# Rewriting a fused attention and expert-routing kernel: batched routing, plain loads, interleaved head pairs, independent scatters

## The chip, the cores and the metric

The kernel runs on one core of one Trainium2 chip. The metric is the device time of one execution in microseconds (us). PE is the matmul engine, PEld its weight loads, ACT the scalar engine, DVE the vector engine, Pool (POOL) the general-purpose engine, SP the engine that only issues DMAs. "Clock" is the share of full speed that was granted to PE, by the clock records of the trace; the time before the first record is counted as 1.00.

## The reference, cut to what matters

Eight batches, eight heads, 576 tokens, head size 64. Each head adds two attentions: a coarse one over means of four tokens, repeated four times, and a local one in which a token sees the seven tokens around it. The result has 4608 rows of 512. Then each row goes through the two-layer network of its domain (one of eight experts).

```python
q_d = q.reshape(B, H, Sd, factor, D).mean(axis=3)           # k_d, v_d alike; factor = 4
out_up = np.repeat(sm_attn(q_d, k_d, v_d), factor, axis=2)
mask = np.abs(pos[:, None] - pos[None, :]) < factor
out_local = softmax(np.where(mask, scale * q @ k.T, -1e9)) @ v
x = (out_up + out_local) as rows of tokens                   # 4608 x 512
for e in range(E):                                           # 8 experts
    m = domain_id == e
    out[m] = np.maximum(x[m] @ w1[e], 0.0) @ w2[e]           # 512 -> 1024 -> 512
```

## The kernel before

Attention works on pairs of heads. It loads q, k and v with converting DMAs from Pool (256 bytes of fp32 become 128 bytes of fp16), loads v once more in overlapping windows, and writes local rows and coarse rows to DRAM. After every second batch a pass reads both back, adds them, and writes the sum.

```python
for src, dst, dstl in ((q, qn, qnl), (k, kn, knl), (v, vq, vql)):
    nc.gpsimd.dma_start(dst[:], src[b, hA:hA+2, 0:512, :].rearrange("h (p r) d -> p r h d", r=4))
    ...
# _od_add_pass, 36 times in all, DMAs issued from ACT
nc.scalar.dma_start(xt[:], xdr[base:base+P, :])
nc.scalar.dma_start(ot[:], odb[srow:srow+32, :].unsqueeze(1).broadcast_to([32, 4, DM]))
nc.vector.tensor_add(xt[:], xt[:], ot[:])
nc.scalar.dma_start(xdr[base:base+P, :], xt[:])
```

Routing computes the place of each token in its expert's list in 36 serial steps on DVE and PE, and 36 indirect DMAs write the list to DRAM. The expert stage has room for 6 x 128 tokens per expert; each block of 128 output rows is scattered to its tokens.

```python
for j in range(CAPJ):                                     # CAPJ = 6
    for fc in range(NFC):
        nc.tensor.matmul(o_ps[:], ht[:, fc, bass.ts(j, P)], w2e[:, fc, :], ...)
    o_sb = msb.tile([P, DM], FP32, name="o_sb", tag="o_sb")       # three buffers
    nc.scalar.copy(out=o_sb[:], in_=o_ps[:])
    nc.gpsimd.indirect_dma_start(out=out[:], out_offset=..idxt[:, j:j+1].., in_=o_sb[:], ...)
```

The softmax here doesn't subtract the row's maximum and nothing guards it: scores larger than these inputs give would overflow.

## Time and profile before

The time before was 688.0 us (median of 4 runs). The stages, read from the timeline of the profiled execution (691.2 us):

| stage | from, to | us |
|---|---|---|
| start, to the first score matmul | 0 to 72.8 | 72.8 |
| attention, to the last local product | to 379.0 | 306.2 |
| hand-over, to the first hidden matmul | to 414.4 | 35.4 |
| experts, to the last output matmul | to 681.2 | 266.8 |
| tail | to 691.2 | 10.0 |

Page of the kernel before, its 40 slices of time: busy tenths of PE, its clock, the mean busy share of the 16 DMA engines, and what they moved.

```profile
PE   1778989876987478866897019793939394867983
PEclk9999999999999999999999999996969788797998
DMA  9990769999999989999313597456565536363411
GB/s 119 180 82 1 56 91 95 158 142 135 118 140 138 157 116 88 119 193 185 41 30 106 134 212 165 102 85 139 97 137 98 122 82 98 110 113 119 92 60 54
```

The same by windows of time. Columns: window, its length, busy time of PE, PEld, DVE, ACT and POOL with instruction counts, clock, DMA share, GB/s.

```profile
68.00:395.00 327.00, 251.01 (x2046) 157.05 (x2045) 204.68 (x866) 161.10 (x378) 186.35 (x248) 1.00 0.91 118
410.00:691.00 281.00, 198.11 (x1087) 103.63 (x1084) 0.00 (x0) 101.77 (x144) 99.05 (x103) 0.87 0.50 106
```

In attention no engine is saturated, but the DMA engines look nearly so. The clock of 1.00 there is not a measurement: the first clock record of this trace lies at 418.5 us. The spacing of matmuls says what the clock was. Two groups of 128-column transposes, in attention and in the experts, and a 512- and a 256-column matmul before and after that record (start us, duration us, engine, line, operation, tile, shapes, count; a wait stands in brackets):

```profile
217.09 0.61 PE L272 MATMUL pdt_ps<-id16a,qn 128*128 128x128 f16 x4
416.91 0.63 PE L445 MATMUL h_ps<-xt,w1e 128*128 128x512 f16 x1
417.34 0.42 PE L449 MATMUL h_ps<-xt,w1e 128*128 128x256 f16 x1
420.04 0.38 PE L445 MATMUL h_ps<-xt,w1e 128*128 128x512 f16 x1
420.25 0.27 PE L449 MATMUL h_ps<-xt,w1e 128*128 128x256 f16 x1
459.42 0.78 PE L433 MATMUL xt_ps<-id,xg 128*128 128x128 f16 x11
```

From one start to the next, 512 columns take 0.43 us at 416.9 and 0.21 us at 420.0. Transposes come every (0.61 - 0.31) / 3 = 100 ns in attention and every (0.78 - 0.22) / 10 = 56 ns in the experts (0.31 and 0.22 us are the durations of a single one). So PE ran at about half clock through all of attention before, and its 251 us of busy time are at half clock. Mean clocks of whole executions and of windows leave this early time out.

In the experts everything has slack, and PE's row goes up and down with its clock. The list of waits of the kernel before says why. Columns: who waited, for whom, total us, times, longest.

```profile
ACT o_sb L463 <- DMA out_dram<-o_sb,idxt: 69.2, 11, 12.7
PE o_ps L458 <- ACT o_sb L463: 69.0, 21, 12.6
POOL xg L416 <- DMA idxt<-hx_idx: 44.0, 5, 9.5
```

The first two lines are one chain: PE waits for the copy of the output block, and the copy waits for a buffer that an earlier scatter still holds. The third is Pool's own wait, for the index loads of the gathers.

### The profile page before, as it was taken

Reading aid. Unit: us, or ns where it says so; the run is one execution under the profiler, and the core shown is the slowest. Engines: PE = TensorE matmul, PEld = TensorE weight load, DVE = VectorE, ACT = ScalarE, POOL = GpSimd, SP = SyncE. Lnnn points to the kernel's source line nnn. Section 1 sums busy time; section 2 is a strip of 40 time slices with the busy share of each in tenths; the row PEclk is TensorE's granted clock in tenths of the full one; section 3 lists DMA queues with packets and bytes.
Section 4 is the critical chain, followed back from the end, with each engine's and each line's share of the span. In section 5 each row is a group of like instructions: output and inputs, shape, how many; then the busy total and the mean of one; then the engine's idle time right before and its main releaser. Section 6 shows DMA issues by size and latency. Waiting matters only on the chain. (4 is left out here: it accounts for less than half of the span.)

```text
span 691.2 us, 10101 instructions
## 1 busy us (share of the span) xinstructions
PE 493.7 (71%) x3352; PEld 300.3 (43%) x3352; DVE 237.3 (34%) x1118; ACT 267.8 (39%) x528; POOL 334.2 (48%) x408
## 2 busy tenths in 40 slices
PE   1778989876987478866897019793939394867983
PEld 1777656543654245534554015441515152433441
DVE  1664455775666656667567100000000000000000
ACT  0100766425763255623764005441424152434441
POOL 9930667775975659954200155124252434243222
PEclk9999999999999999999999999996969788797998
DMA  9990769999999989999313597456565536363411
GB/s 119 180 82 1 56 91 95 158 142 135 118 140 138 157 116 88 119 193 185 41 30 106 134 212 165 102 85 139 97 137 98 122 82 98 110 113 119 92 60 54
DMA packets 226905, 77.93 MB, mean 113 GB/s; under 512 B 196609, under 2 KB 218898, under 8 KB 226836
## 3 DMA queue, kind: packets, MB, share of 16 engines
q0 software_dynamic: 133504, 46.71, 55.4%
q1 hardware_dynamic: 72100, 15.23, 12.8%
q10 hardware_dynamic: 21248, 15.35, 7.8%
q8 instruction: 26, 0.43, 0.3%
q14 instruction: 27, 0.22, 0.2%
HBM read 88.09 MB, written 23.37 MB: 161 GB/s over the span
## 5 line engine op out<-in xcount | busy, mean ns | idle before, releaser
L458 PE MATMUL o_ps<-w2e,ht 128*128 128x512 f16 x384 | 100.1, 407 | 70.3 <-ACT o_sb L463 69.0
L464 POOL DMA_INDIRECT out_dram<-o_sb,idxt x48 | 47.3, 986 | 120.4 <-ACT o_sb L463 40.8
L458 PEld LDWEIGHTS <-ht 128*128 128x128 f16 x384 | 39.5, 103 | 119.5 <-issue 87.4
L445 PE MATMUL h_ps<-xt,w1e 128*128 128x512 f16 x256 | 88.8, 394 | 1.9 <-ACT xt L438 1.0
L463 ACT COPY o_sb<-o_ps 128x512 f32<-128x512 f32 x48 | 28.1, 585 | 137.7 <-DMA out_dram<-o_sb,idxt 69.2
L416 POOL DMA_INDIRECT xg<-hx_bridge,idxt x48 | 46.3, 964 | 60.7 <-DMA idxt<-hx_idx 44.0
L449 PE MATMUL h_ps<-xt,w1e 128*128 128x256 f16 x256 | 72.0, 281 | 0.0
L230 POOL DMA_DIRECT2D qn<-in_q_dram x32 | 48.4, 1512 | 36.5 <-PE pdtl_ps L274 23.7
L230 POOL DMA_DIRECT2D vq<-in_v_dram x32 | 58.5, 1840 | 13.4 <-DVE pos_s L125 8.6
L453 ACT ACTIVATE ht<-h_ps 128x768 f16<-128x768 f32 x64 | 51.7, 811 | 28.8 <-PE h_ps L449 28.7
L149 POOL DMA_INDIRECT hx_idx<-tok_s,pos_s x36 | 37.6, 1044 | 50.1 <-DMA hx_idx<-tok_s,pos_s 45.3
L330 ACT ACTIVATE el<-sc_ps 128x640 f16<-128x640 f32 x64 | 44.7, 703 | 23.4 <-PE sc_ps L313 12.0
L230 POOL DMA_DIRECT2D kn<-in_k_dram x32 | 50.2, 1569 | 3.7 <-PE pdtl_ps L274 3.2
L313 PE MATMUL sc_ps<-qt,kt 64*128 64x128 f16 x320 | 45.4, 303 | 9.2 <-POOL kt L268 4.6
L262 ACT COPY qt<-tr_ps 128x512 f16<-128x512 f16 x24 | 31.1, 1297 | 28.8 <-PE tr_ps L260 28.8
L234 POOL DMA_DIRECT2D vql<-in_v_dram x32 | 41.8, 1306 | 1.0 <-DVE vdl L287 0.8
L234 POOL DMA_DIRECT2D knl<-in_k_dram x32 | 40.9, 1278 | 0.0
L445 PEld LDWEIGHTS <-w1e 128*128 128x128 f16 x256 | 25.9, 101 | 32.6 <-issue 4.3
L249 ACT CAST vh<-vn 128x640 f16<-128x640 f32 x32 | 23.1, 727 | 40.6 <-DVE vn L247 21.3
L433 PE MATMUL xt_ps<-id,xg 128*128 128x128 f16 x192 | 15.7, 230 | 31.5 <-DMA xg<-hx_bridge,idxt 31.5
L438 ACT COPY xt<-xt_ps 128x768 f16<-128x768 f16 x32 | 24.0, 815 | 36.0 <-PE xt_ps L433 36.0
L234 POOL DMA_DIRECT2D qnl<-in_q_dram x32 | 36.9, 1152 | 0.7 <-PE pdtl_ps L274 0.7
(88 smaller groups left out, 1041.5 us busy)
## 6 DMA issues: line engine op xcount, KB each, us to landing
vn<-in_v_dram SPq DMA_DIRECT2D x64, 128.0 KB
w1e<-in_moe_w_dram POOLq DMA_DIRECT2D x8, 1024.0 KB
w2e<-in_moe_w_dram POOLq DMA_DIRECT2D x8, 1024.0 KB
oax<-hx_bridge ACTq DMA_DIRECT2D x36, 128.0 KB
hx_bridge<-oax ACTq DMA_DIRECT2D x36, 128.0 KB
qn<-in_q_dram POOLq DMA_DIRECT2D x32, 128.0 KB
kn<-in_k_dram POOLq DMA_DIRECT2D x32, 128.0 KB
vq<-in_v_dram POOLq DMA_DIRECT2D x32, 128.0 KB
```

The lines of the kernel that those rows point to most:

```text
L149: nc.gpsimd.indirect_dma_start(out=idxd[:], out_offset=bass.IndirectOffsetOnAxis(ap=pos_s[:, t : t + 1], axis=0), in_=tok_s[:, t : t + 1], ...
L230: nc.gpsimd.dma_start(dst[:], src[b, hA : hA + 2, 0:512, :].rearrange("h (p r) d -> p r h d", r=4),)
L234: nc.gpsimd.dma_start(dstl[:], src[b, hA : hA + 2, 512:S, :].rearrange("h (p r) d -> p r h d", r=4),)
L262: nc.any.tensor_copy(tt[:, 0:512].rearrange("w (p r) -> w r p", r=4), ps_m[:])
L313: nc.tensor.matmul(sc_ps[hh][:, t, :], kt[rs : rs + 64, 120 * t : 120 * t + P], qt[rs : rs + 64, 120 * t : 120 * t + P], start=True, stop= ...
L330: nc.scalar.activation(out=el[hh][:], in_=sc_ps[hh][:], func=AF.Exp, scale=scale_local)
L416: nc.gpsimd.indirect_dma_start(out=xg[:, j, :], out_offset=None, in_=xdr[:], in_offset=bass.IndirectOffsetOnAxis(ap=idxt[:, j : j + 1], ax ...
L445: nc.tensor.matmul(h_ps[:, 0:512], lhs, xt[:, dc, 0:512], start=(dc == 0), stop=(dc == NDC - 1),)
L449: nc.tensor.matmul(h_ps[:, 512:NCOL], lhs, xt[:, dc, 512:NCOL], start=(dc == 0), stop=(dc == NDC - 1),)
L453: nc.scalar.activation(out=ht[:, fc, :], in_=h_ps[:], func=AF.Relu)
L458: nc.tensor.matmul(o_ps[:], ht[:, fc, bass.ts(j, P)], w2e[:, fc, :], start=(fc == 0), stop=(fc == NFC - 1),)
L464: nc.gpsimd.indirect_dma_start(out=out[:], out_offset=bass.IndirectOffsetOnAxis(ap=idxt[:, j : j + 1], axis=0), in_=o_sb[:], in_offset=Non ...
```

## The change

Nearly the whole kernel was rewritten. The intents were to take small and serial DMA work away, to interleave the PE work of several pairs in a fixed order, and to let scatters overlap. The core of the diff, with cuts:

```diff
-CAPJ = 6
+CAPJ = 5
-for t in range(NT):                       # 36 serial routing steps, 36 index scatters
-    ...
-    nc.gpsimd.indirect_dma_start(out=idxd[:], ..., in_=tok_s[:, t:t+1])
+nc.vector.tensor_tensor_scan(cs, rst, oh, 0.0, ALU.mult, ALU.add)       # all tokens at once
+for t in range(NT):                       # the list by one-hot products, stays in SBUF
+    nc.tensor.matmul(ips[:], ol[:, t, :], rh[:, t], start=(t == 0), stop=(t == NT - 1))
-    nc.gpsimd.dma_start(dst[:], src[...])                   # converting, 256 B -> 128 B
+    nc.sync.dma_start(t[...], src[b, h0:h0+4].rearrange("h (p r) d -> p h (r d)", r=6))  # plain, 1536 B
+    nc.gpsimd.tensor_scalar(dst, src[:], 1.0, 1.0, op0=ALU.mult, op1=ALU.mult)           # cast on Pool
-        nc.vector.tensor_mul(pl[hh][:], el[hh][:], mask5_s[:])
+                nc.tensor.matmul(s[:, 0:512], ident, off.unsqueeze(1).broadcast_to([P, 4, P]), ...)
+                nc.tensor.matmul(s[:, 512:640], ident, off, ...)        # mask added by PE
-            if b % 2 == 1:
-                _od_add_pass(nc, xdr, odb, b - 1, S, SD, DM, asb)
+            nc.tensor.matmul(t[:], upm[:, w, :], nrm[b][:, :, ...])      # coarse rows, repeated by PE
+            nc.vector.tensor_tensor(out=xw[b][:, w], in0=t, in1=nrm[b][:, :, w, :], op=ALU.add)
+        with tc.manual_schedule(engines={PE, Activation, DVE, Pool, SP}):
+            for i in range(NPAIR + 1):
+                j = i - 1
+                pe_sc(i); exp_sc(i, 0); exp_sc(i, 1)           # scores of pair i
+                pe_av(j, 0); norm(j, 0)                        # products of pair i - 1
+                pe_tr(i + 2, 0); ...; pe_tr(i + 2, 1); evac_tr(i + 2)   # transposes of pair i + 2
+                pe_av(j, 1); norm(j, 1)
+                ...
+                    ob = msb.tile([P, DM], FP32, name="ob", tag="ob", bufs=8)
+                    sc = nc.gpsimd.indirect_dma_start(out=out[:], ...)
+                    tc.declare_no_dep(sc.ins, group="scatter",
+                                      reason="scatters write disjoint rows")
```

It also keeps three sets of weights instead of two; two are loaded before attention ends.

## The prediction

> **What bounds the kernel now.** The table by time windows shows two stages: attention to about 395 us, experts from 410 to 691 us.
>
> *Attention (68 to 395 us).* The DMA engines are busy 0.91 of the time but move only 118 GB/s: the page counts 196,609 of 226,905 packets under 512 B. The converting q, k, v loads on the software queue take most of it (55.4% of 16 engines' span for 133,504 packets: 46 ns each; the plain SP queue, 12.8% for 72,100: 20 ns). This agrees with the Trainium skill, "DMA: Bandwidth & Descriptors", Specifications, which puts line rate at 512 B and up. PE is busy 251 of 327 us. Cadence: about 10 us per head pair.
>
> *Experts (410 to 691 us).* PE is busy 198 of 281 us at a granted clock of 0.87. In the list of waits, PE waits 69 us for the output copy, which waits 69 us for earlier scatters: these run one after another, 3.5 us apart in the chain that ended last. The gaps drop the clock to 0.50 (470 to 480, 510 to 520, 620 to 630 us); it returns to 1.00 in dense stretches, as the skill's "TensorE: Matmul & The Clock Gate", Part 1, describes.
>
> **What the change does.**
> - Routing in one batch instead of 36 serial steps and 36 index scatters.
> - q and k loaded plain in 1.5 KB rows and cast by Pool; v loaded once; window mask added by PE; coarse rows added from PSUM, not through DRAM: no 36 read-add-write passes.
> - Fixed program order, PE work of three pairs interleaved.
> - Capacity 640 instead of 768 per expert (this draw: at most 625), 1/6 less PE work; scatters independent, eight output buffers, three weight sets, two loaded before attention ends.
>
> **Cost, estimated from durations in the trace.**
> - Start: constants, first loads, routing on DVE: 22 us.
> - Attention, PE per pair: spacing in the trace is 55 to 60 ns for 128x65 and transposes, 100 ns for 64-row scores, 107 ns for accumulating transposes, 150 ns where row counts alternate, 216 ns for 512 columns. About 77 matmuls give 5.3 to 7 us; I take 6.1. ACT: two exps of 928 (0.95 us each, from 0.70 for 640) and one strided evacuation of 1152 (1.2 to 2.7) = 3.1 to 4.6 us. DVE: about 3 us. DMA: 41k packets of 256 B at 20 ns and 19 MB in long packets, about 130 us in all. So PE bounds it: 32 x 6.1 = 195 us.
> - Hand-over: last coarse adds, store, first gathers (1.25 us each, 2.7 to land): 18 us.
> - Experts, PE: 64 matmuls of 320 columns (0.136), 40 of 512 (0.216), 20 transposes (0.06) = 18.6 us; times 8 = 149. ACT, DVE and Pool (10 indirect transfers at 1.25, loads 2) stay under 16 us each.
> - Tail: copy, last scatter: 7 us.
>
> Sum 391 us. Nearly all of the saving is on the critical path: about 175 us in attention with its start, 120 us in the experts.
>
> **Predicted: 390 us, range 355 to 440.** Chances: faster 0.985, within 2% 0.01, slower 0.005.
>
> **What would show it.** Right: PE busy over 85% in both stages; experts 150 to 165 us at a clock above 0.95, no wait of the output copy on scatters; DMA share under 0.8 in attention; cadence 5.3 to 7 us. Wrong: PE waiting in attention for ACT's evacuation, Pool's casts or loads; scatters or weight loads delaying the experts.
>
> **What would make it wrong.** PE's mixed row counts and mask matmuls costing more than here (cadence 8 us: +60 us); Pool's casts, of which the trace has no example, far slower than ACT's 0.73 us per 640 elements; single-buffered PSUM tiles stalling PE; two-byte constant writes delaying the first loads; weights arriving late behind scatters.

## The result and the profile after

| | before | after |
|---|---|---|
| median us | 690.3 (15 runs) | 362.57 (10 runs) |
| ratio of fast runs | | 0.5241, interval 0.5221 to 0.5261 |
| result | correct | correct |

Ratios here are the mean time of one kernel's fast runs over that of the other's of the same rounds, so they are not quite the ratio of the medians quoted. Three of the ten runs after (367 to 370 us) and one before (895.6 us) are not used for them.

The stages beside the terms of the prediction. "Control" is the same kernel again, in the last group of experiments:

| stage, us | before | predicted | after | control |
|---|---|---|---|---|
| start | 72.8 | 22 | 26.0 | 26.0 |
| attention | 306.2 | 195 | 151.2 | 149.1 |
| hand-over | 35.4 | 18 | 19.2 | 19.2 |
| experts | 266.8 | 149 | 157.9 | 151.2 |
| tail | 10.0 | 7 | 6.3 | 6.3 |
| sum | 691.2 | 391 | 360.6 | 351.8 |

Page of the kernel after, the rows that answer to those above (here a slice is 9 us, not 17):

```profile
PE   0077998999999999899414999899989898998993
PEclk9999998999999999999655899999999999999998
DMA  5999999999999999989923893997979697981202
GB/s 88 229 204 201 225 220 227 225 249 222 239 198 265 208 258 214 243 153 219 214 67 102 157 191 111 163 251 144 233 169 211 182 187 225 170 239 60 113 29 103
```

The same by windows, attention and experts:

```profile
28.00:174.00 146.00, 134.77 (x2283) 95.37 (x2279) 94.12 (x205) 90.44 (x94) 64.87 (x54) 0.99 1.08 223
197.00:350.00 153.00, 145.29 (x952) 87.88 (x952) 40.72 (x68) 44.15 (x69) 78.05 (x81) 0.99 0.76 167
```

PE is busy 92% of attention and 95% of the experts, at a clock of 0.99 (about 0.97 in attention, an estimate that counts its first 6 us, before the first record, as half). The DMA engines move 223 instead of 118 GB/s in attention and still show a share over 1. More matmuls than before (2283 against 2046) take about half of PE's busy time, at twice the clock.

The timeline of the kernel after, one head pair on PE. Columns: start us, duration us, engine, line, operation, tile, shapes, count.

```profile
111.45 0.38 PE L266 MATMUL sc<-c_s 128*128 128x512 f16 x1
111.67 0.22 PE L269 MATMUL sc<-c_s 128*128 128x128 f16 x1
111.73 0.38 PE L266 MATMUL sc<-c_s 128*128 128x512 f16 x1
111.94 0.22 PE L269 MATMUL sc<-c_s 128*128 128x128 f16 x1
112.09 0.46 PE L276 MATMUL sc<-qkt 64*128 64x128 f16 x10
112.39 0.29 PE L281 MATMUL sc<-qkd 64*128 64x144 f16 x4
112.61 0.33 PE L309 MATMUL av<-vh,el 128*128 128x65 f16 x5
112.77 0.59 PE L314 MATMUL av<-vd,el 128*128 128x65 f16 x4
113.30 0.56 PE L224 MATMUL tr<-c_s,qkh 96*128 96x96 f16 x9
...
114.04 0.76 PE L234 MATMUL tr<-c_s,qkh 96*128 96x48 f16 x24
114.64 0.31 PE L309 MATMUL av<-vh,el 128*128 128x65 f16 x5
114.80 0.59 PE L314 MATMUL av<-vd,el 128*128 128x65 f16 x4
...
115.55 0.38 PE L266 MATMUL sc<-c_s 128*128 128x512 f16 x1
```

From mask to mask of the next pair it is 4.10 us, without one wait (a wait would stand in brackets at the end of a line). Spacing within a group is its duration less that of one matmul, over the count less one: 24 pooling matmuls (0.76 - 0.185) / 23 = 25 ns, ten scores (0.46 - 0.22) / 9 = 27 ns (two heads run at once: single records of the trace start in pairs, one of each head, about 4 ns apart, and a pair follows every 55 to 65 ns), nine transposes 44 ns, five local products 35 ns, four coarse products of changing row counts 130 ns. The coarse pooling of v adds 1.6 us per batch.

In the experts, the chain of waits on scatters is gone. What is left of PE's waits there is a stall of 0.7 to 1.4 us in seven of the eight experts. The timeline of the kernel after shows it, hidden-layer matmuls of two experts:

```profile
217.42 7.77 PE L458 MATMUL hp<-xt,w1e 128*128 128x320 f16 x56
226.57 1.25 PE L458 MATMUL hp<-xt,w1e 128*128 128x320 f16 x8 [1.39 <-DVE ht L466]
237.40 7.82 PE L458 MATMUL hp<-xt,w1e 128*128 128x320 f16 x56
245.91 1.25 PE L458 MATMUL hp<-xt,w1e 128*128 128x320 f16 x8 [0.68 <-DVE ht L466]
```

### The profile page after: what moved, and what is told of

It reads as the page before. It is cut to its first block, busy times and chain, and to the rows that moved or that the text cites. A ratio compares the mean times of both kernels' runs of the same rounds, so it can differ in the third digit from the quotient of the medians.

```text
span 360.6 us, 7965 instructions
## 1 busy us (share of the span) xinstructions
PE 301.7 (84%) x3422; PEld 196.7 (55%) x3422; DVE 156.2 (43%) x308; ACT 142.6 (40%) x170; POOL 157.6 (44%) x155
## 3 DMA queue, kind: packets, MB, share of 16 engines
q1 hardware_dynamic: 64112, 34.84, 46.1%
## 4 chain that ended last, share of the span: by engine, by line
PE 50%; DMA 14%; issue 11%; POOL 10%; DVE 6%; SPq 6%; ACT 1%; POOLq 1%; DVEq 0%; ACTq 0%
PE op L472 12%; PE hp L458 11%; DMA qkf<-in_k_dram 10%; PE av L314 6%; POOL qkh L353 4%; PE tr L224 4%; PE tr L234 4%; POOL out_dram L477 3%; POOL xg L430 3%; PE up L333 3%; SPq L129 3%; PE av L309 2%; PE sc L266 2%; DMA out_dram<-ob,idx 2%; PE sc L276 2%
## 5 line engine op out<-in xcount | busy, mean ns | idle before, releaser
L458 PE MATMUL hp<-xt,w1e 128*128 128x320 f16 x512 | 74.4, 304 | 7.8 <-DVE ht L466 4.8
L472 PE MATMUL op<-w2e,ht 128*128 128x512 f16 x320 | 74.9, 379 | 0.0
L353 POOL TENSOR_SCALAR qkh<-qkf 96x3072 f16<-96x3072 f32 x15 | 41.2, 2749 | 71.3 <-DMA qkf<-in_k_dram 39.3
L477 POOL DMA_INDIRECT out_dram<-ob,idx x40 | 39.6, 991 | 67.5 <-ACT ob L475 67.5
L288 ACT ACTIVATE el<-sc 128x928 f16<-128x928 f32 x64 | 56.9, 941 | 26.6 <-PE sc L281 26.6
L430 POOL DMA_INDIRECT xg<-x_rows,idx x40 | 38.6, 964 | 40.3 <-DMA x_rows<-xw 28.4
L252 ACT COPY qkt<-tr 128x1152 f16<-128x1152 f16 x32 | 35.8, 1118 | 33.5 <-PE tr L234 26.2
L325 DVE TENSOR_TENSOR nrm<-av,rc 128x448 f16<-128x448 f32 x64 | 40.0, 625 | 2.2
L314 PE MATMUL av<-vd,el 128*128 128x65 f16 (+1 forms) x256 | 38.8, 200 | 2.4 <-DVE vd L298 2.4
L224 PE MATMUL tr<-c_s,qkh 96*128 96x96 f16 x384 | 27.9, 213 | 8.7 <-POOL qkh L353 6.0
```

The source lines that it names most:

```text
L224: nc.tensor.transpose(t[:, TRS * r:TRS * r + 96], qkh[u][:, r, h0:h0 + 2, :].rearrange("p h d -> p (h d)"), ident[0:96, 0:96])
L252: nc.scalar.copy(out=a[:], in_=src)
L288: nc.scalar.activation(out=el[i][:, h, :], in_=sct.pop((i, h))[:], func=AF.Exp, scale=scale)
L314: nc.tensor.matmul(t[:, NW + n, :], el[i][p0:P, h, c:c + P], vd[p0:P, m, hh, :], start=(m == 0), stop=(m == 1), skip_group_check=True)
L325: nc.vector.tensor_tensor(out=nrm[b][:, hh], in0=t[:, :, 0:D], in1=rc[:].broadcast_to([P, 7, D]), op=ALU.mult)
L353: nc.gpsimd.tensor_scalar(dst, src[:], 1.0, 1.0, op0=ALU.mult, op1=ALU.mult)
```

## The experiments

Twelve kernels ran, in three groups of four. Runs of one group are on one chip with shared runs of the kernel before; the groups were on different chips.

### 1. One part alone, in the kernel before: independent scatters

```diff
-        o_sb = msb.tile([P, DM], FP32, name="o_sb", tag="o_sb")
+        o_sb = msb.tile([P, DM], FP32, name="o_sb", tag="o_sb", bufs=8)
-        nc.gpsimd.indirect_dma_start(
+        sc = nc.gpsimd.indirect_dma_start(
...
+        tc.declare_no_dep(sc.ins, group="scatter", reason="scatters write disjoint rows")
+        tc.add_to_no_dep_group("scatter", sc.ins)
```

> The kernel before, with one part of the change alone: scatters declared independent and eight output buffers. Theory (serial scatters bound the expert stage, PE waits 69 us and the clock falls to 0.5): the stage from the first gather transposes to the end shrinks from 281 us to about 200 to 215, granted clock of the stage from 0.87 to over 0.95, total about 610 to 625 us. Rival (gathers, their index loads and Pool's order hold PE as well, 44 us of waits on index loads): the waits only change their name and the total stays above 650 us. Result stays correct.

Measured 621.49 us, ratio 0.8989 (0.8931 to 0.9047), correct. Attention is nearly unchanged (the last score matmul starts at 373.3 instead of 376.4 us); nearly all of the 70 us come from the experts, where the clock rose from 0.87 to 0.99 (410 us to the end). The theory of serial scatters holds, and its rival falls: waits on the index loads stay (52 us on Pool in this run), but cost PE nothing that shows in the total.

### 2. Is attention before bound by the small converting loads?

```diff
-    for src, dst, dstl in ((q, qn, qnl), (k, kn, knl), (v, vq, vql)):
+    vq, vql = kn, knl
+    for src, dst, dstl in ((q, qn, qnl), (k, kn, knl)):
```

> The kernel before without the second, converting load of v (the coarse values are computed from k: wrong on purpose). It takes away a third of the small converting packets and of Pool's load issues in attention, about 36,900 packets. Theory of the prediction (attention is bound by the converting DMA loads): attention shortens by a good part of a third, 60 us or more, total below 630 us. Rival (loads run four to five pairs ahead of their use; the order of work on PE, ACT and DVE and their waits set the pace): attention shortens by less than 20 us.

Measured 679.42 us, ratio 0.9815 (0.9749 to 0.988). Its output is wrong, which doesn't matter for the time. The window of attention of this run, to be read against the first window of the kernel before:

```profile
68.00:395.00 327.00, 252.23 (x2055) 158.26 (x2055) 204.47 (x866) 160.24 (x378) 146.77 (x206) 1.00 0.78 117
```

Read this line against 251.01, 0.91 and 118 of the kernel before. The DMA share fell by 0.13 and Pool's busy time by 40 us, because a third of the converting loads is gone. PE did its work in the same time, and attention ended only 16 us earlier in the profile (the last score matmul starts at 360.8 instead of 376.4 us). A third of a load that bounded a stage of 306 us should have given far more. The converting loads do take most of the DMA share, as the prediction says; but its reading of that share as what bounds attention before falls, and the rival (less than 20 us) holds: a DMA share of 0.91 was not a bound.

### 3. Is it the read-add-write passes?

```diff
-            if b % 2 == 1:
-                _od_add_pass(nc, xdr, odb, b - 1, S, SD, DM, asb)
```

> The kernel before without the 36 read-add-write passes that add the coarse rows through DRAM (wrong on purpose). Theory of the prediction (bandwidth): they move 14 MB, worth at most 25 us of DMA time. Rival: their DMAs are issued from ACT and ACT stands still in order behind them (about 40 us of ACT waits on these tiles in the list of waits), and the last ones hold up the first gathers after attention: 35 to 70 us less, the gap of PE between attention and experts among it.

Measured 661.27 us, ratio 0.9568 (0.9506 to 0.9629): 30 us less. Its output is wrong, which doesn't matter for the time. In the profile the last score matmul is 22 us earlier (354.5 us) and the first transpose of a gathered block 33 us earlier (376.5 instead of 409.7 us). So about two thirds of it is in attention and one third in the hand-over, where the last passes ran. The number lies just above what the one theory allowed and 5 us under the other's range; the run does not decide whether the passes cost bandwidth or hold up ACT, which issues their DMAs in order with the exps. What it shows is that the passes are the largest single part of attention before that any run found.

### 4. The change without the declaration that scatters are independent

```diff
-                    tc.declare_no_dep(sc.ins, group="scatter",
-                                      reason="scatters write disjoint rows")
-                    tc.add_to_no_dep_group("scatter", sc.ins)
```

> The kernel after with the scatters ordered again (no declaration of independence; eight buffers stay). Theory: 40 scatters at about 3.5 us each are 140 us, which Pool must issue among 40 gathers of 1.25 us and the weight loads, so Pool's chain passes PE's 19.8 us per expert: 5 x 3.5 + 5 x 1.25 + 2 = about 26 us per expert, 45 us more in all, total about 400 to 420 us, PE clock of the expert stage below 0.95. Rival (eight buffers hide the order): less than 10 us more.

Measured 442.3 us, ratio 0.6403 (0.6359 to 0.6446), correct: 80 us more than the change, and so worse than expected. From the fourth expert on, experts start every 33.7 us instead of every 20.0. The list of waits of this run, experts only (who waited, for whom, total us, times, longest), and the window of its experts:

```profile
PEld L439 <- DMA xg<-x_rows,idx: 68.3, 6, 13.5
PE xt_ps L439 <- DMA xg<-x_rows,idx: 66.3, 6, 13.1
POOL out_dram L477 <- issue: 59.8, 20, 12.4
```

```profile
197.00:430.00 233.00, 162.19 (x966) 93.43 (x964) 41.14 (x67) 45.90 (x72) 78.58 (x83) 0.84 0.50 112
```

Output buffers are plentiful here (eight), so PE does not wait for a copy as in the kernel before. It waits for the next expert's gathers, which stand on the same Pool queue behind scatters that run one by one. 66 us of waits and a clock of 0.84 instead of 0.99 make the 80 us. Independent scatters matter twice: they free buffers, and they let the gathers through.

### 5. Does PE set the pace of attention before?

The ten local score matmuls of each pair are issued twice, into the same place.

```diff
+        for t in range(NSPAN):
+            nc.tensor.matmul(
+                sc_ps[hh][:, t, :],
+                kt[rs : rs + 64, 120 * t : 120 * t + P],
+                qt[rs : rs + 64, 120 * t : 120 * t + P],
+                start=True, stop=True)
```

> The kernel before with its local score matmuls issued twice (same result): 320 more matmuls of 64 rows at the 100 ns that their spacing shows, 32 us of PE work in attention. Theory (after the second-v run fell: PE's own in-order work and its short waits set the pace of attention before): 20 to 35 us longer. Rival (DMA or Pool set the pace, PE has slack of 76 us in attention): under 10 us longer.

Measured 703.34 us, ratio 1.011 (1.0052 to 1.0169), correct: 8 us more. The same window as above:

```profile
68.00:395.00 327.00, 285.56 (x2366) 190.49 (x2365) 205.65 (x859) 163.99 (x380) 186.67 (x247) 1.00 0.88 113
```

PE is busy 34.5 us more, and three quarters of it disappears in idle time. The theory that PE sets the pace falls. (The 1.00 is again time without a record: the first lies at 429.6 us, and scores last 311 ns at the median.)

### 6. Does ACT set the pace of attention before?

```diff
+        nc.scalar.activation(out=el[hh][:], in_=sc_ps[hh][:], func=AF.Exp,
+                             scale=scale_local)
```

> The kernel before with the local exponential issued twice (same result): 64 more ACT instructions of 0.70 us, 45 us of ACT work in attention, where ACT is busy 161 of 327 us. Theory (PE sets the pace, the other engines have slack): under 15 us longer. Rival (the chain score, exponential, mask, product within one head pair sets the pace, so that latency on any engine counts): 25 to 45 us longer.

Measured 705.41 us, ratio 1.0163 (1.0099 to 1.0226), correct: 11 us more. The second exp takes 44 us of ACT, but the window shows that the program answered:

```profile
68.00:395.00 327.00, 251.34 (x2045) 157.47 (x2044) 232.09 (x913) 168.44 (x391) 185.90 (x247) 1.00 0.88 114
```

ACT is only 7 us busier and DVE 27 us: copies whose engine is chosen when the program is built went from ACT to DVE. The test is weakened by that, though 44 us were still added to one engine's exps. Taken together, runs 2, 3, 5 and 6 say that in attention before neither the loads (12 us for a third of them), nor PE (8 for 34), nor ACT (11 for 44) alone sets the pace. The add passes (30 us) are a part. The rest is most likely many short waits between engines that each work in order; that is argued, not shown, and stays open. In all four runs PE stayed at half clock in attention, as in the kernel before (scores of 311 ns; first clock records at 386 to 430 us), so none of them tests what that clock costs.

### 7. Was the interleaving of heads what made the scores cheap?

The prediction took 100 ns per score matmul; the change shows 27. This run issues all scores of one head, then all of the other, as the kernel before does.

```diff
-            for w in range(NW + 2):
-                for h, s in enumerate(ss):
+            for h, s in enumerate(ss):
+                for w in range(NW + 2):
```

> The kernel after with the score matmuls of the two heads one head after the other instead of alternating between the two halves of the rows (same result). The kernel before shows 100 ns between such matmuls when all use the same half, the kernel after 30 ns when they alternate. Theory (PE sets the pace of attention after, and alternation is one reason why a pair takes 4.6 and not the predicted 6.1 us): 448 matmuls times about 70 ns, 20 to 35 us longer. Rival (DMA sets the pace of attention after, its share is 1.08): under 8 us longer.

Measured 357.5 us, ratio 0.5121 (0.5069 to 0.5174), correct; one of its four runs is slow (366 us) and left out. The unchanged kernel in the next group has 0.517 (0.5131 to 0.521): the intervals overlap, so no difference is shown, and 20 to 35 us can be ruled out. In the profile the score phase of a pair does grow, from 0.52 to 0.70 us, 40 instead of 27 ns each: about 6 us of PE time over 32 pairs, and the first hidden matmul starts 4 us later than in that unchanged kernel (198.7 against 194.4 us). So alternating heads is worth little: the timeline shows scores of the second head starting before those of the first have ended, so two heads still run partly at once. The 100 ns of the kernel before were spacing within one head at half clock. In the kernel after it is twice 27 or 54 ns within a head, and in stretches of run 10 at half clock, with the same alternation, ten scores last 0.72 us: (0.72 - 0.31) / 9 = 45 ns, 91 within a head.

### 8. Do loads set the pace of attention after?

Only three units of q and k and two batches of v are loaded; the others reuse those tiles.

```diff
-                        qkf[u + 3] = load_qk(u + 3)
+                        qkf[u + 3] = qks[u % 3]
-                        vn[b + 2] = load_v(b + 2)
+                        vn[b + 2] = vns[b % 2]
```

> The kernel after, loading q and k only for the first three units and v only for the first two batches and computing all others from those tiles (wrong on purpose): about 24 of 29 MB of loads fall away, work of the engines stays the same. Theory (PE sets the pace of attention after): at most 8 us shorter. Rival (the loads set it, DMA share 1.08 over the stage): attention shrinks by 20 us or more.

Measured 347.07 us, ratio 0.498 (0.4946 to 0.5015), wrong on purpose. That is 10 us less than run 7 on the same chip, and by the ratios 13 us less than the unchanged kernel. The window of attention, to be read against the second window of the kernel after:

```profile
28.00:174.00 146.00, 136.34 (x2308) 96.25 (x2303) 96.99 (x212) 90.48 (x94) 63.83 (x54) 0.98 0.35 72
```

The DMA share falls from 1.08 to 0.35, yet PE is as busy as before, 136 instead of 135 us of 146. The last score matmul starts at 163.4 us, instead of 168.5 in the unchanged kernel of run 9 and 170.4 in the first profile. So 5 to 7 us of attention are due to loads. The whole profiles differ by 6 us (345.7 against 351.8 us in run 9), less than the 13 by ratios, which compare two chips. The total is a little over what the theory of PE expected and well under its rival. PE's own work sets the pace after the change, with loads close behind, even where the share column says 1.08.

### 9. Control: the kernel after, unchanged

> The kernel after once more, unchanged, as the control of this call and to see whether the stall of 1.4 us at the last block of hidden units of seven experts, which its profile shows and the two variants of the call before do not, belongs to the program or to that execution. Program: stage from first hidden matmul to last scatter issue again about 159 us, total 360 to 364 us. Execution or chip: about 151 us, total 350 to 357 us.

Measured 355.3 us, ratio 0.517 (0.5131 to 0.521), correct. Its timeline, hidden-layer matmuls of two experts that follow each other:

```profile
215.93 8.86 PE L458 MATMUL hp<-xt,w1e 128*128 128x320 f16 x64
234.37 8.90 PE L458 MATMUL hp<-xt,w1e 128*128 128x320 f16 x64
```

All 64 hidden matmuls of an expert run in one group; in the first profile of the kernel after they were split 56 and 8, with a wait of 0.7 to 1.4 us between. Experts come every 18.5 instead of 20.0 us, and the stage takes 151.2 instead of 157.9 us. The profiles of runs 4, 7, 8 and 10 to 12 do not have the stall either. It belongs to that execution or that chip, not to the program; what made ACT or DVE late there stays open.

### 10. The same instructions without interleaving

Transposes, evacuation, scores, exps and products of one pair follow each other, and then comes the next pair. Not an instruction is added or removed.

```diff
-                if i < NPAIR:
-                    pe_sc(i)
-                    exp_sc(i, 0)
-                    exp_sc(i, 1)
-                if j >= 0:
-                    pe_av(j, 0)
-                    norm(j, 0)
-                if i + 2 < NPAIR:
-                    pe_tr(i + 2, 0)
...
+                pe_tr(i, 0); pe_tr(i, 1); evac_tr(i)
+                pe_sc(i); exp_sc(i, 0); exp_sc(i, 1)
...
+                pe_av(i, 0); norm(i, 0)
...
+                pe_av(i, 1); norm(i, 1)
```

> The kernel after with the attention work of one pair after another in program order (transposes, evacuation, scores, exponentials, products of the same pair) instead of work of three pairs interleaved; same instructions, same result. Theory (fixed interleaving is what lets PE set the pace; within one pair each step waits for another engine: evacuation 1.1 and 0.45 us, exponential 0.94 us, normalisation 0.8 us and the hand-overs between them): a pair takes 7.5 to 9 us instead of 4.6, attention 95 to 140 us longer, total 450 to 500 us, DMA share of attention far below 1. Rival (less and cheaper PE work is what counts, queues overlap pairs anyway): under 40 us longer.

Measured 480.59 us, ratio 0.6976 (0.6925 to 0.7027), correct: 125 us more than the control on the same chip. Attention takes 281.7 instead of 149.1 us. Its window, the waits of PE in it, and two groups of its timeline:

```profile
23.00:304.00 281.00, 212.00 (x2351) 136.31 (x2349) 98.85 (x209) 92.41 (x96) 65.31 (x54) 0.63 0.61 123
```

```profile
PE av L309 <- ACT el L288: 26.1, 24, 1.1
PE av L309 <- DVE nrm L325: 24.0, 32, 1.0
PE sc L276 <- ACT qkt L252: 7.3, 30, 0.7
```

```profile
101.75 1.16 PE L234 MATMUL tr<-c_s,qkh 96*128 96x48 f16 x24
102.74 0.60 PE L266 MATMUL sc<-c_s 128*128 128x512 f16 x1
```

The waits listed, with two more of 6.3 and 4.8 us, come to about 69 us, where the kernel after has 11. The larger part of the 133 us is the clock: PE is busy 212 us with the work that took 135, because the clock is 0.63 in this stage, and the same 24 pooling matmuls take 1.16 instead of 0.76 us, the 512-column mask 0.60 instead of 0.38. No single wait of these is longer than 1.1 us. The Trainium skill, "TensorE: Matmul & The Clock Gate", section "Why this matters for your kernels", asks for no idle gap over about 3 us; here far shorter ones were enough. Its Part 1, "A second HAM failure mode", does tell of a kernel whose clock suffered from very short idle times between groups of matmuls, and this run agrees with that. So the order is worth two things: the waits it hides, and the clock that they would cost.

### 11. A faster start

The first group of q and k is loaded before the constants, a constant written in two-byte pieces by DMA is copied by Pool instead, the exp table is loaded early, and routing moves into iterations 4 to 14 of attention. The last coarse adds also get more PSUM buffers.

```diff
-        vd = con.tile([P, 2, H, D + 1], FP16, name=f"vd{n}")
-        nc.sync.dma_start(vd[:, :, :, D:D + 1], ones1_c[:])
+        nc.gpsimd.tensor_copy(vd[:, :, :, D:D + 1], c16[:, 1760:1776]...)
+    nc.scalar.activation(out=warm[:], in_=warm[:], func=AF.Exp)
...
-    with (tc.tile_pool(name="rsb", bufs=1) as rsb, ...):     # routing ahead of attention
+        def r_a(): ...                                       # the same steps, called from the pair loop
```

> Meant to beat the kernel after: first q and k loads ahead of all constants, the two-byte constant writes replaced by a copy on Pool, the routing work on DVE moved from the start into iterations 4 to 14 of attention, last coarse adds in four PSUM buffers instead of one. Same result. Theory (PE is without dense work for 28 us at the start and 23 us at the hand-over): 6 to 14 us faster than the control of this call. Rival (the start is bound by the bytes of the first loads, and routing on DVE disturbs attention): within 3 us of the control.

Measured 358.46 us, ratio 0.5217 (0.5191 to 0.5243), correct: no gain, 3 us more than the control. The first score matmul starts at 17.6 instead of 26.0 us, but the first hidden matmul at 200.7 instead of 194.4 us. The two windows of this run's attention, with routing in the first:

```profile
40.00:110.00 70.00, 57.36 (x865) 39.96 (x866) 49.75 (x95) 31.52 (x33) 32.57 (x23) 0.85 1.02 216
110.00:180.00 70.00, 67.73 (x1161) 48.03 (x1160) 49.86 (x109) 46.01 (x49) 26.09 (x25) 1.00 1.01 209
```

In equal time PE does 865 matmuls in the first and 1161 in the second. In the first, PE waits 4.7 us once for a cast on Pool, 4.3 us in five parts for normalisations on DVE and 3.2 us before two routing matmuls, and the clock is 0.85. The routing steps on DVE stand in order before the normalisations; that they are the cause of the rest is argued, as the run changed several things at once. The start was saved and attention paid for it.

### 12. Mask on DVE and Pool, not on PE

On top of run 11, the window mask multiplies the exps, head 0 on DVE and head 1 on Pool, and the four mask matmuls of a pair go.

```diff
-                nc.tensor.matmul(s[:, 0:512], ident,
-                                 off.unsqueeze(1).broadcast_to([P, 4, P]), start=True, stop=False, ...)
-                nc.tensor.matmul(s[:, 512:640], ident, off, start=True, stop=False, ...)
+            def mul(eng):
+                eng.tensor_tensor(out=e, in0=e, in1=off.unsqueeze(1).broadcast_to([P, NW, P]),
+                                  op=ALU.mult)
```

> As the run before, and in addition the window mask applied by multiplying after the exponential, one head on DVE and one on Pool, instead of by four PE matmuls per pair (same result). It takes 0.55 us of PE work per pair away, 17 us in all, and gives DVE about 0.5 us and Pool about 1.3 us per pair. Theory (PE sets the pace of attention): 8 to 15 us faster than the run before. Rival (the loads, DMA share 1.08, or DVE and Pool take over at once): within 4 us of it, or slower.

Measured 404.44 us, ratio 0.5882 (0.5856 to 0.5908), correct: 46 us more than run 11, where 8 to 15 less were expected. The window of its attention:

```profile
20.00:224.00 204.00, 174.03 (x2180) 124.42 (x2177) 130.14 (x252) 88.36 (x93) 110.46 (x87) 0.65 0.83 168
```

PE has less to do and takes longer. The multiply (749 ns on DVE, 1460 ns on Pool) now stands between exp and product, PE waits 14.9 us for DVE's, at most 2.1 us at a time, and the clock is 0.65 (about 0.58, an estimate that counts the time before the first record at 49.5 us as half: pooling groups last 1.16 us there). A mask that costs PE about 0.54 us per pair (two 512-column matmuls of 216 ns, two of 56) was cheaper here than the waits and the clock that moving it cost. None of my versions beats the kernel after.

## Why the prediction was right, and where it was wrong

The total is right: 390 us predicted, 362.6 measured, inside the range of 355 to 440 and near its low end. In part that is luck: attention was put 44 us too high, and the range was wide enough to hold it. Nor did the prediction say that the clock of attention would double; run 10, where the clock of attention is 0.63, takes 480.6 us, outside the range. By stages the change saved 46.8 us at the start, 155.0 in attention, 16.2 at the hand-over, 108.9 in the experts and 3.7 in the tail. The prediction put about 175 us on attention with its start (202 measured) and 120 on the experts (109).

- **Experts: right.** 149 us predicted, 157.9 in the first profile and 151 in the control. The cause is right too: run 1 gains 70 us from independent scatters alone, run 4 loses 80 without them. The clock came back as the prediction said, from 0.87 to 0.99. PE is busy 95%, and no output copy waits for a scatter.
- **Start, hand-over, tail: right** within 4 us each (22, 18 and 7 against 26.0, 19.2 and 6.3).
- **Attention, size: wrong.** The step was "100 ns for 64-row scores, 107 ns for accumulating transposes, 150 ns where row counts alternate", which gave 6.1 us per pair, 195 us in all. Measured were 27, 25 and 130 ns, 44 for transposes and 35 for local products; only the 216 ns of 512 columns held. The pooling group alone falls from 2.6 (24 x 107 ns) to 0.6 us, the scores of 14 matmuls from 1.4 to 0.4. A pair takes 4.7 us on average (151.2 / 32), under the predicted 5.3 to 7. The costs that failed were read in attention before, where PE ran at half clock, and were summed with 216 ns, which was read in the experts at full clock. Two of them were also of other work: 107 ns belong to 128 columns, and the new pooling matmuls have 48 (38 ns at half clock in run 10, (1.16 - 0.28) / 23); 100 ns belong to one head, and in the new order two run at once. Where row counts alternate, 130 instead of 150 ns, the clock made little difference. Run 7 shows that the order of heads counts for little.
- **Attention, bound after: right in kind.** PE bounds it, as predicted: it is busy 92%, and run 8 gains no more than 5 to 7 us in attention by leaving nearly all loads out.
- **"DMA share under 0.8 in attention": wrong.** It is 1.08. The term was 20 ns per small packet, read from a queue with little load. After the change the page gives 46.1% of 16 engines' span for 64,112 packets of that queue: 0.461 x 16 x 360.6 us / 64,112 = 41 ns each, long packets included. Run 8 shows that the high share nonetheless hardly costs time.
- **"The converting q, k, v loads on the software queue take most of it", as what bounds attention before: wrong.** They do take most of the DMA share, but run 2 takes a third of them away and gains 12 us. No single engine or queue that the runs tried sets the pace of attention before (runs 2, 3, 5, 6), and the prediction missed that PE ran at half clock there. Its saving for attention came from the costs of the new kernel, not from this account of the old one.
- **Feared and not met.** Pool's casts take 2.75 us per 3072 elements, faster per element than the ACT copy they were measured against. PE's list of waits after has none for weights behind scatters, and its mask matmuls cost what their columns say.

What carried the gain in attention is the order. Run 10 has all the smaller loads, batched routing and PSUM adds of the change, and only not its interleaving: attention takes 281.7 us there and 306.2 in the kernel before. And the order works through the clock as well as through the waits: attention ran at half clock before, at 0.63 in run 10 and at about 0.97 after. Why PE stayed at half clock in attention before (its waits of up to 4.6 us, its many small gaps or its other mix of matmuls) no run tests.

## What to carry to other kernels

A high busy share is a suspicion, not a bound: take a part of the suspected work away, and believe it only if time follows; here a share of 0.91 gave 12 us for a third of its load, and one of 1.08 gave 5 to 7 us of attention for nearly all of it. A spacing holds the clock at which it was read, and a clock of 1.00 may be time without a record: compare a matmul of known size in two stretches (here 512 columns every 0.43 or 0.21 us) before you take costs from one. Where PE bounds a stage, fill its order with work of other pairs before moving work off it: waits of about 1 us, with the lower clock that came with them, cost 133 us, and a multiply moved from PE to engines in its chain cost 46 us.

## What the Trainium skill lacked or had wrong

- "TensorE: Matmul & The Clock Gate", "Why this matters for your kernels": its rule (no idle gaps over about 3 us) is not enough. The clock was 0.63 over 281 us with waits of at most 1.1 us (run 10), and about 0.58 over 204 us with a single wait of more than 2.9 us, one of 4.3 (run 12). Part 1, "A second HAM failure mode", tells of the case but gives no length of the idle times. The kernel before stayed at half clock through 306 us of attention with PE busy 77% of it, run 10 with 75% at 0.63; what share or length of gaps decides stays open.
- No page says that a trace can have no clock record before the first change of the clock. Here 418 us of the kernel before have none and are shown as 1.00, though attention ran at half clock (512 columns every 0.43 us just before the first record, 0.21 after).
- "TensorE: Matmul & The Clock Gate", Part 2, "Back-to-back issue gap": it gives about 81 ns (128 columns) and 131 ns (512 columns) for streams in which weights are loaded too, and calls 56 and 216 ns figures of isolated matmuls. Here 512 columns came every (1.89 - 0.38) / 7 = 216 ns and 128-column transposes of the experts every (0.39 - 0.22) / 3 = 57 ns in a dense kernel; 24 matmuls of 48 columns ran at 25 ns, the floor that the page names.
- "DMA: Bandwidth & Descriptors", Specifications, puts line rate at 512 B and up. Nothing here contradicts it, but removing a third of the converting loads (37,888 packets under 512 B fewer) gave only 12 us. No page gives the price of indirect scatters that wait for each other (this one has a cost per DMA of Pool's path, not for this case): they were 3.5 us apart in the kernel before, and 70 us of 690 in all (run 1).
- "GPSIMD Engine Reference", 3.1, puts the cost of a two-input operation at about 2.6 cycles per element and down to reading two inputs. The trace agrees as far as it goes: a one-input cast of 3072 elements took 2747 ns, and a two-input multiply of 640 elements 1460 ns, which per element is 2.5 times the cast.
- No page has a stall that comes with the execution and not with the program: 0.7 to 1.4 us in seven experts of the first profile after, none in those of runs 4 and 7 to 12.
